# Lead-in of layer B: V tails staged in two tiles and stored by four transfers on SP, Q/K tails stored on SP alone

## The chip, the cores and the metric

The kernel runs on one core of one Trainium2 chip. The time is the device time of one execution in microseconds (us). The engines are TensorE (PE; its weight loads are shown apart as PEld), VectorE (DVE), ScalarE (ACT), GpSimd (POOL) and SyncE (SP). SP and ACT each have a queue on which they issue transfers (DMAs); the profile shows these as SPq and ACTq.

## What is computed

Four layers in a row, A, B, A, B, over 2048 tokens of width 640, each added to its input after a layernorm. This change touches only B, a recurrent attention with a memory of eight tokens:

```python
def _B_ref(x, mem0, Wq, Wk, Wv, Wo, seg_len):          # seg_len 32, 32 heads of 128
    mem = mem0                                           # 8 tokens
    for s in range(n_seg):                               # 64 segments
        xs = x[:, s * seg_len:(s + 1) * seg_len, :].copy()
        h = jnp.concatenate([mem, xs], axis=1)           # 40 tokens
        q, k, v = (einsum('btd,dhe->bhte', h, W) for W in (Wq, Wk, Wv))
        scores = einsum('bhqe,bhke->bhqk', q, k) * scale
        scores = jnp.where(mask[None, None], scores, -1000000000.0)
        o = einsum('bhqk,bhke->bhqe', softmax(scores), v)
        o = einsum('bhte,hed->btd', o, Wo)
        mem = o[:, :M, :].copy()                         # the next segment's memory
        outs.append(o[:, M:, :])
```

## The kernel before

Layer B (`layer_B`) works through 64 steps, one per segment, and each step needs the memory that the one before it made. A step multiplies 32 columns at a time: the eight memory tokens together with the first 24 tokens of the segment ("thin" products, `thin_mm`). The last eight tokens of each segment, the tails, don't depend on the memory. Their queries, keys and values are therefore made ahead, for eight segments at once, by sixteen units: eight for Q and K (`tail_unit`, `tail_evac`), eight for V (`vtail_unit`, `vtail_evac`). ACT or DVE evacuates a unit from PSUM into a staging tile in SBUF; the unit is then stored in DRAM, Q and K tails in `b_QKd`, V tails in `b_VTd`, and each step loads what it needs back, in the layout it needs: `b_tl` by one load (`tails_load`), which POOL then copies into `b_QZ` and `b_KT` (`tails_copy`), and the V tails by four loads into rows of `b_Vth` (`vtails_in`).

In the steady loop the units of the next eight segments are spread over eight steps. Ahead of the loop there is a lead-in (lines 983 to 1034), run once in each of the two B layers, that does all sixteen units of the first eight segments in a row:

- the layernorm of four groups of 128 tokens (`ln_load`, `ln_norm`), and their transposition into `b_HX` and `b_TX` (`ln_spread`: five transposes on PE into `b_lntps`, two copies on ACT);
- the eight Q/K units on PSUM tile `b_tail` (lines 997 to 1004), even ones evacuated by ACT and odd ones by DVE into `b_tu`, which stands in turn in four buffers of `b_kq` and in `b_QT`, `b_KT`, `b_tu` and `b_Vth`; even units are stored by ACT's queue, odd ones by SP's; `ln_spread` of the groups 2 and 3 stands after units 3 and 5;
- the thin products of step 0 (`b_Kp`, `b_Qp`), eight loads of the output weights `b_wo` on SP (640 KB each, line 1014), the transposes `b_TP`;
- the load of `b_tl` for step 0 (line 1021), which has to wait for all eight stores to `b_QKd`;
- the eight V units on PSUM tile `b_vtail` (lines 1024 to 1026), even ones evacuated by DVE and stored by SP, odd ones evacuated by ACT and stored by ACT; five are staged in one tile `b_vts` (the memory of `b_OTsb`), three in `b_vt` (the memory of `b_PTa`, `b_PTb` and `b_E`); each unit is stored by two transfers of 64 rows of 512 bytes;
- the thin product for V (`b_V`), the four loads of V tails into `b_Vth` (line 1030), and the first units of the next eight segments (lines 1032 to 1034).

Then step 0 begins with the thin products of step 1 (`b_Ka`, `b_Qa`, `b_Kb`, `b_Qb`), the transposes (`b_TPak` and so on), the scores of step 0 (`b_SP`), softmax, the product with V (`b_OTP`, which reads `b_Vth`) and the output projection (`b_OPS`, which reads `b_wo`).

The order on each engine is that of the program text: `_OrdNC` chains the instructions of PE, ACT, DVE and POOL, and ACT's stores stand in ACT's own order. SP's order is chosen by the scheduler of the framework. PSUM tiles of the lead-in share five buffers that go round (`ps_tile`), so a product may start only when the tile five before it has been evacuated. The framework gives every transfer of SP and ACT one of eight semaphores in turn; before a transfer is issued its queue waits until the last transfer with the same semaphore has landed.

`OTdef` are two tiles of 128 x 32 x 32 in which POOL collects the memory rows of `b_OTsb` at the end of every step, four steps per tile.

Of the kernel before, what the change touches and what calls it, by code (L numbers as in the profile page):

```python
# [19 lines left out]
BF16 = mybir.dt.bfloat16  # L20
# [756 lines left out]
def layer_B(nc, tc, C, W, x_src, xb_src, x_dst, mem0, B_Wv, B_Wo, nsteps=64, out_bf16=False, tag=""):  # L777
    SCB = 1.0 / math.sqrt(128.0)
    nc_raw = nc
    nc = _OrdNC(tc, nc_raw, engines=ORDER_ENGINES)  # L780
# [3 lines left out]
    VTd = tc.dram_tile([nsteps, 8, 4096], BF16, name=f"b_VTd{tag}")  # L784
    with ExitStack() as ctx:
        def pool(name, bufs):
            return ctx.enter_context(tc.tile_pool(name=name, bufs=bufs, reuse_waits="tile"))
# [6 lines left out]
        kqp = pool("b_kqp", 4)  # L794
        W.wo = pool("b_wo", 1).tile([128, 32, D], BF16, name="b_wo")
        st = pool("b_state", 1)
        w2 = pool("b_w2", 2)
        wk = pool("b_wk", 1)
# [8 lines left out]
        def ps_tile(shape, dtype, name):  # L807
            return pp.tile(shape, dtype, name=name, tag="ps")
# [7 lines left out]
        OTdef = [wk.tile([128, 32, 32], BF16, name=f"b_OTdef{i}") for i in range(2)]  # L816
# [12 lines left out]
        HX, TX, QT, KT, VH = {}, {}, {}, {}, {}  # L829
        ln_xt, ln_ready = {}, []  # L830

        def evac(eng, dst, src, scale=None):
            if eng == "act":
                if scale is None:
                    nc.scalar.copy(dst, src)
                else:
                    nc.scalar.activation(out=dst, in_=src, func=ACT.Copy, scale=scale)
            else:
                if scale is None:
                    nc.vector.tensor_copy(dst, src)  # L840
                else:
                    nc.vector.tensor_scalar(out=dst, in0=src, scalar1=scale, scalar2=None, op0=ALU.mult)
# [7 lines left out]
        def ln_norm(g):  # L850
            xt = ln_xt[g]
            f = layernorm_tile(nc, sml, C, xt[:], xt[:], "b_ln")
            if g in (0, 2) and not entered:
                info = mybir.DependencyInfo(mybir.DependencyClass.NoSync, mybir.DependencyReason.SCHED_ONLY)
                tc.add_manual_dep(f.ins, (C.after2 if g else C.after).ins.name, info, reason="order")
            ln_ready.append(g)

        def ln_spread(g):
            xt = ln_xt.pop(g)
            tps = ps_tile([128, NCH, 4, 32], BF16, "b_lntps")  # L860
            for c in range(NCH):
                nc.tensor.transpose(tps[:, c, :, :].rearrange("p i t -> p (i t)"), xt[:, 128 * c:128 * c + 128], C.identb[:])
            HX[g] = hp.tile([128, NCH, 4, 32], BF16, name="b_HX", tag="HX")
            T, half = divmod(g, 2)
            if half == 0:
                TX[T] = tx.tile([128, NCH, 8, 8], BF16, name="b_TX", tag="TX")
            nc.scalar.copy(TX[T][:, :, 4 * half:4 * half + 4, :], tps[:, :, :, 24:32])
            nc.scalar.copy(HX[g][:, :, :, 8:32], tps[:, :, :, 0:24])

        def cols_of(u):  # L870
            if u == nsteps:
                return HXz[:, :, 0, :]
            return HX[u // 4][:, :, u % 4, :]

        def thin_mm(cols_ap, Wt, b, name):
            ps = ps_tile([128, 512], F32, name)
            for c in range(NCH):
                for j in range(4):
                    n = 4 * b + j
                    nc.tensor.matmul(ps[32 * j:32 * j + 32, :], lhsT=cols_ap[:, c, :], rhs=Wt[:, c, 512 * n:512 * n + 512],  # L880
                                     start=(c == 0), stop=(c == NCH - 1), tile_position=(0, 32 * j), skip_group_check=True)
            return ps
# [30 lines left out]
                nc.sync.dma_start(VH[s - 1][32 * j:32 * j + 8, :, :],  # L913
                                  VTd[s].rearrange("t (b n e) -> t n b e", b=2, e=512)[:, j, :, :])

        tail_ps, vts = {}, {}

        def tail_unit(T, k, i0, i1, shared=False):
            proj, hg = divmod(k, 4)
            Wt = W.wk if proj else W.wq  # L920
            if i0 == 0:
                if shared:
                    tail_ps[0] = ps_tile([128, 8, 64], F32, "b_tail")
                else:
                    tail_ps[0] = po.tile([128, 8, 64], F32, name="b_tail", tag="tail")
            ps = tail_ps[0]
            for i in range(i0, i1):
                h = 8 * hg + i
                for c in range(NCH):
                    nc.tensor.matmul(ps[:, i, :], lhsT=Wt[:, c, 128 * h:128 * h + 128], rhs=TX[T][:, c, :, :].rearrange("p s t -> p (s t)"),  # L930
                                     start=(c == 0), stop=(c == NCH - 1))

        def tail_evac(T, k, eng, home=None, dma=nc.sync.dma_start):
            proj, hg = divmod(k, 4)
            pool_, tg = home or (wk, "tu")
            tu = pool_.tile([128, 8, 8, 8], BF16, name="b_tu", tag=tg)
            evac(eng, tu[:].rearrange("p s h t -> p h s t"), tail_ps[0][:].rearrange("p h (s t) -> p h s t", t=8),
                 None if proj else SCB)
            o = 256 * proj + 64 * hg
            dma(QKd[8 * T:8 * T + 8, :, o:o + 64].rearrange("s p f -> p s f"), tu[:].rearrange("p s h t -> p s (h t)"))  # L940

        def vtail_unit(T, k, c0=0, c1=NCH, ps=None):
            b4, ch = divmod(k, 2)
            if ps is None:
                ps = ps_tile([128, 256], F32, "b_vtail")
            for c in range(c0, c1):
                for q in range(4):
                    n = 2 * b4 + q // 2
                    nc.tensor.matmul(ps[32 * q:32 * q + 32, :], lhsT=TX[T][:, c, 4 * (q % 2):4 * (q % 2) + 4, :].rearrange("p s t -> p (s t)"),
                                     rhs=W.wv[:, c, 512 * n + 256 * ch:512 * n + 256 * ch + 256],  # L950
                                     start=(c == 0), stop=(c == NCH - 1), tile_position=(0, 32 * q), skip_group_check=True)
            return ps

        def vtail_evac(T, k, ps, eng, home=None, dma=nc.sync.dma_start):
            b4, ch = divmod(k, 2)
            if isinstance(home, int):
                if home == 0:
                    vts[0] = wk.tile([128, 5, 256], BF16, name="b_vts", tag="OTsb")
                vt = vts[0][:, home, :]
            else:  # L960
                pool_, tg = home or (wk, "vt")
                vt = pool_.tile([128, 256], BF16, name="b_vt", tag=tg)[:]
            evac(eng, vt, ps[:])
            for jj in range(2):
                o = 512 * (2 * b4 + jj) + 256 * ch
                dma(VTd[8 * T:8 * T + 8, :, o:o + 256].rearrange("s t f -> (s t) f"), vt[64 * jj:64 * jj + 64])
# [29 lines left out]
                nc.sync.dma_start(HX[0][:, c, 1, 0:8], mem0[:, 128 * c:128 * c + 128].rearrange("t p -> p t"))  # L996
        for k in range(8):
            tail_unit(0, k, 0, 8, shared=True)
            tail_evac(0, k, "act" if k % 2 == 0 else "dve", (((kqp, "kq"),) * 4 + ((w2, "QT"), (w2, "KT"), (wk, "tu"), (w2, "Vth")))[k],
                      (nc.sync if k % 2 else nc.scalar).dma_start)  # L1000
            if k in (0, 2) and n0 > 2:
                ln_norm(2 + k // 2)
            if k in (3, 5) and ln_ready:
                ln_spread(ln_ready.pop(0))
        cols = cols_of(0)
        jobs = [(nm, b) for b in range(2) for nm in ("K", "Q")]
# [1 line left out]
        for nm, b in jobs:  # L1008
            ps = thin_mm(cols, W.wk if nm == "K" else W.wq, b, f"b_{nm}p")
# [10 lines left out]
        XO, XOd = init_state()  # L1020
        tails_copy(0, tails_load(0))
        Vth = VH[-1] = w2.tile([128, 2, 512], BF16, name="b_Vth", tag="Vth")
        vt_homes = [0, 1, 2, 3, 4] + [(wk, x) for x in ("PTa", "PTb", "E0")]
        for k in range(8):
            vtail_evac(0, k, vtail_unit(0, k), "dve" if k % 2 == 0 else "act", vt_homes[k],
                       (nc.scalar if k % 2 else nc.sync).dma_start)
        for b in range(2):
            ps = thin_mm(cols, W.wv, b, "b_V")
            evac("act" if b == 0 else "dve", Vth[:, b, :], ps[:])
        vtails_in(0)  # L1030
        if NT > 1:
            tail_unit(1, 0, 0, 8, shared=True)
            tail_evac(1, 0, "act")
            vtail_evac(1, 0, vtail_unit(1, 0), "dve")
# [52 lines left out]
        for s in range(nsteps):  # L1087
# [139 lines left out]
            PTa = wk.tile([128, 2, 4, 40], BF16, name="b_PTa", tag="PTa")  # L1227
            ptpb = p_transp(1)
            PTb = wk.tile([128, 2, 4, 40], BF16, name="b_PTb", tag="PTb")
# [10 lines left out]
            OTsb = wk.tile([128, 32 * 40], BF16, name="b_OTsb", tag="OTsb")  # L1240
# [30 lines left out]
            if not last:  # L1271
                dst = cols_of(u + 1)
# [14 lines left out]
            if unit:  # L1287
                vtail_evac(unit[0], unit[1], vps, "act")
# [113 lines left out]
```

## Time and profile before

| what | value |
|---|---|
| median of the three runs shown | 2696.44 us (2691.12 to 2700.09) |
| the profiled execution's own time | 2692.14 us |
| its span in the profile | 2690.4 us |
| mean granted PE clock | 0.997 |
| PE busy | 2576.7 us, 96% of the span |
| DMA moved | 156.37 MB, mean 58 GB/s |

The page gives, for one profiled execution, the busy time of each engine, the chain of work that ended last, and the costliest groups. The timeline view lists instructions as "start us, us, engine, line, operation, out<-in, count", and in brackets the time the engine stood idle ahead of them and what ended it. The two B layers begin near 343 us and 1683 us of the span; their lead-ins end near 382 and 1722 us, where `b_Ka` of the loop begins. Line numbers of helpers stand for many instructions (L109 is the recorder through which nearly all of B's instructions go), so the tile names are what to go by.

### The profile page before, as it was taken

Reading aid. Unit: us, or ns where it says so; the run is one execution under the profiler, and the core shown is the slowest. Engines: PE = TensorE matmul, PEld = TensorE weight load, DVE = VectorE, ACT = ScalarE, POOL = GpSimd, SP = SyncE. Lnnn points to the kernel's source line nnn. Section 1 sums busy time; section 2 is a strip of 40 time slices with the busy share of each in tenths; the row PEclk is TensorE's granted clock in tenths of the full one; section 3 lists DMA queues with packets and bytes.
Section 4 is the critical chain, followed back from the end, with each engine's and each line's share of the span. In section 5 each row is a group of like instructions: output and inputs, shape, how many; then the busy total and the mean of one; then the engine's idle time right before and its main releaser. Section 6 shows DMA issues by size and latency. Waiting matters only on the chain.

```text
span 2690.4 us, 147288 instructions
## 1 busy us (share of the span) xinstructions
PE 2576.7 (96%) x65632; PEld 1699.2 (63%) x65632; DVE 1698.4 (63%) x4562; ACT 1583.1 (59%) x3718; POOL 710.0 (26%) x1631
## 2 busy tenths in 40 slices
PE   7999989999999999999989999899999999999998
PEld 5556566666666666666655566666666666666665
DVE  8999845555555555555589998455555555555554
ACT  6988835454555555554479898355555555555543
POOL 5777611111111111111156776111111111111110
PEclk9999999999999999999999999999999999999999
DMA  4122451222222222121120113511212121211110
GB/s 155 45 79 80 139 166 41 44 44 43 44 45 43 45 43 44 41 41 31 54 89 22 61 51 138 164 40 40 43 39 44 41 43 41 42 40 41 38 26 19
DMA packets 326620, 156.37 MB, mean 58 GB/s; under 512 B 246240, under 2 KB 310880, under 8 KB 324192
## 3 DMA queue, kind: packets, MB, share of 16 engines
q1 hardware_dynamic: 316384, 145.38, 21.3%
q8 instruction: 513, 8.40, 1.4%
q10 hardware_dynamic: 9600, 1.57, 0.4%
q14 instruction: 123, 1.01, 0.1%
HBM read 95.15 MB, written 51.71 MB: 55 GB/s over the span
## 4 chain that ended last, share of the span: by engine, by line
PE 79%; DVE 11%; ACT 5%; DMA 2%; issue 2%; SPq 1%; POOL 0%; ACTq 0%; DVEq 0%; POOLq 0%
PE b_OPS L109 11%; PE b_tail L109 5%; DVE a_nm L138 5%; PE b_Qa L109 5%; PE b_Ka L109 5%; PE b_Kb L109 5%; PE b_Qb L109 5%; PE b_Va L109 5%; PE b_Vb L109 5%; PE b_SP L109 4%; PE b_OTP L109 4%; PE b_OPSd L109 3%; PE b_PTP L109 3%; PE b_vtail L109 3%; ACT a_PT L138 3%; PE a_S L109 2%
## 5 line engine op out<-in xcount | busy, mean ns | idle before, releaser
L109 PEld LDWEIGHTS <-b_HX 128*32 128x32 bf16 x15360 | 427.9, 97 | 343.0 <-issue 12.4
L109 POOL TENSOR_TENSOR b_Pm<-b_E,b_rs 128x96 bf16<-128x96 bf16 x128 | 63.6, 497 | 1430.7 <-ACT b_Vth L109 1079.3
L138 DVE TENSOR_REDUCE a_nm<-a_S 128x2 f32<-128x512 f32 (+3 forms) x512 | 394.9, 815 | 27.6 <-PE a_S L109 20.1
L138 ACT ACTIVATE a_PT<-a_T 128x1024 bf16<-128x1024 f32 (+1 forms) x384 | 344.3, 901 | 32.0 <-PE a_T L109 24.2
L109 PE MATMUL b_OPS<-b_wo,b_OTsb 128*32 128x320 bf16 x8192 | 309.5, 301 | 10.4 <-issue 7.6
L109 PEld LDWEIGHTS <-b_OTsb 128*32 128x32 bf16 x8192 | 202.0, 97 | 95.7 <-DVE b_OTsb L109 24.3
L109 DVE CAST b_HX<-b_MT 128x8 bf16<-128x8 f32 x372 | 63.8, 172 | 274.2 <-PE b_MT L109 269.3
L138 POOL TENSOR_SCALAR_AFFINE_SELECT a_PT<-a_PT 128x256 bf16<-128x256 bf16 x380 | 188.7, 505 | 128.5 <-ACT a_PT L138 127.2
L109 ACT CAST b_msb<-b_OPS 128x64 bf16<-128x64 f32 x378 | 69.4, 256 | 237.7 <-PE b_OPS L109 237.6
L109 ACT CAST b_kq<-b_Kb 128x512 bf16<-128x512 f32 x128 | 75.0, 586 | 202.6 <-PE b_Kb L109 202.6
L109 DVE COPY b_KT<-b_TPak 128x128 bf16<-128x128 bf16 x128 | 28.8, 225 | 228.8 <-PE b_TPak L109 228.8
L109 DVE TENSOR_SCALAR b_kq<-b_Qa 128x512 bf16<-128x512 f32 x128 | 88.6, 692 | 130.3 <-PE b_Qa L109 127.2
L109 PE MATMUL b_Ka<-b_wk,b_HX 128*32 128x512 bf16 x2520 | 160.1, 381 | 6.2 <-ACT b_vt L109 6.2
L109 PE MATMUL b_Va<-b_wv,b_HX 128*32 128x512 bf16 x2520 | 161.0, 380 | 0.0
L109 PE MATMUL b_Qa<-b_wq,b_HX 128*32 128x512 bf16 x2520 | 159.9, 381 | 1.1 <-ACT b_Vth L109 1.1
L109 PEld LDWEIGHTS <-b_kq 128*128 128x128 bf16 x2080 | 116.9, 98 | 68.8 <-ACT b_kq L109 55.6
L109 PE MATMUL b_Vb<-b_wv,b_HX 128*32 128x512 bf16 x2520 | 160.3, 379 | 0.0
L109 PE MATMUL b_Kb<-b_wk,b_HX 128*32 128x512 bf16 x2520 | 159.5, 380 | 0.0
L109 PE MATMUL b_Qb<-b_wq,b_HX 128*32 128x512 bf16 x2520 | 158.8, 379 | 0.0
L109 DVE CAST b_OTsb<-b_OTP 128x160 bf16<-128x160 f32 (+1 forms) x384 | 122.5, 374 | 39.7 <-PE b_OTP L109 39.5
L109 ACT ACTIVATE b_E<-b_SP 128x320 bf16<-128x320 f32 (+1 forms) x256 | 81.1, 368 | 108.8 <-PE b_Va L109 100.0
L109 PE MATMUL b_vtail<-b_wv,b_TX 128*32 128x256 bf16 x2880 | 136.9, 271 | 3.9 <-issue 3.9
(211 smaller groups left out, 5786.1 us busy)
## 6 DMA issues: line engine op xcount, KB each, us to landing
b_tl<-b_QKd SPq DMA_DIRECT2D x128, 128.0 KB
b_QKd<-b_tu SPq DMA_DIRECT2D x120, 128.0 KB
b_wv<-in_B_Wv_dram SPq DMA_DIRECT2D x10, 1024.0 KB
b_wo<-in_B_Wo_dram SPq DMA_DIRECT2D x16, 640.0 KB
b_Vth<-b_VTd SPq DMA_DIRECT2D x512, 16.0 KB
b_XO<-xres SPq DMA_DIRECT2D x256, 30.0 KB
b_VTd<-b_vt SPq DMA_DIRECT2D x228, 32.0 KB
xres<-a_xnew SPq DMA_DIRECT2D x19, 320.0 KB
```

Of the source, the lines that this page charges most:

```text
L109: r = f(*a, **k)
L138: r = f(*a, **k)
```

## The change

Three things, all in the lead-in:

1. V tails: units 0 to 3 are staged in `OTdef[0]` and units 4 to 7 in `OTdef[1]`, each in its quarter of 256 columns. After units 3 and 7 two transfers of 64 rows (two pieces of 1024 bytes per row) are issued on SP: four stores of 64 KB in all. The tiles `b_vts` and the borrowed homes go.
2. Q/K tails: all eight stores are issued on SP. ACT issues no transfers any more.
3. `ln_spread` of the groups 2 and 3 stands after units 5 and 7.

In the built program SP's order in the lead-in becomes: one load of `b_wo`, the eight `b_QKd` stores, seven loads of `b_wo`, the load of `b_tl`, the four V stores, the load of `b_tl` for step 1, the first `b_QKd` store of the next eight segments, the four loads of `b_Vth`, the two V stores of that next unit, then two loads each of `b_XO` and `b_XOd`. Before, it was: one `b_wo`, two `b_QKd`, one `b_wo`, one `b_QKd`, one `b_wo`, one `b_QKd`, five `b_wo`, `b_tl`, eight V stores, `b_tl`, one `b_XO`, four `b_Vth`, one `b_QKd`, two V stores, one `b_XO`, two `b_XOd`; in the second B layer the three single `b_wo` stand a little differently among the four `b_QKd`. The orders of DVE and POOL don't change but for the names of the tiles; PE's differs only by the two groups of transposes.

```diff
-        tail_ps, vts = {}, {}
+        tail_ps = {}
...
         def vtail_evac(T, k, ps, eng, home=None, dma=nc.sync.dma_start):
             b4, ch = divmod(k, 2)
-            if isinstance(home, int):
-                if home == 0:
-                    vts[0] = wk.tile([128, 5, 256], BF16, name="b_vts", tag="OTsb")
-                vt = vts[0][:, home, :]
-            else:
-                pool_, tg = home or (wk, "vt")
-                vt = pool_.tile([128, 256], BF16, name="b_vt", tag=tg)[:]
+            if home is not None:
+                vt = OTdef[k // 4][:].rearrange("p a c -> p (a c)").rearrange("p (k f) -> p k f", f=256)[:, k % 4]
+                evac(eng, vt, ps[:])
+                if k % 4 == 3:
+                    src = OTdef[k // 4][:].rearrange("p a c -> p (a c)").rearrange("p (b f) -> p b f", f=512)
+                    dst = VTd[0:8, :, 512 * (k - 3):512 * (k + 1)].rearrange("s t (b j f) -> j (s t) b f", b=2, j=2)
+                    for jj in range(2):
+                        nc.sync.dma_start(dst[jj], src[64 * jj:64 * jj + 64])
+                return
+            vt = wk.tile([128, 256], BF16, name="b_vt", tag="vt")[:]
             evac(eng, vt, ps[:])
...
             tail_unit(0, k, 0, 8, shared=True)
-            tail_evac(0, k, "act" if k % 2 == 0 else "dve", (((kqp, "kq"),) * 4 + ((w2, "QT"), (w2, "KT"), (wk, "tu"), (w2, "Vth")))[k],
-                      (nc.sync if k % 2 else nc.scalar).dma_start)
+            tail_evac(0, k, "act" if k % 2 == 0 else "dve", (((kqp, "kq"),) * 4 + ((w2, "QT"), (w2, "KT"), (wk, "tu"), (w2, "Vth")))[k])
             if k in (0, 2) and n0 > 2:
                 ln_norm(2 + k // 2)
-            if k in (3, 5) and ln_ready:
+            if k in (5, 7) and ln_ready:
                 ln_spread(ln_ready.pop(0))
...
-        vt_homes = [0, 1, 2, 3, 4] + [(wk, x) for x in ("PTa", "PTb", "E0")]
         for k in range(8):
-            vtail_evac(0, k, vtail_unit(0, k), "dve" if k % 2 == 0 else "act", vt_homes[k],
-                       (nc.scalar if k % 2 else nc.sync).dma_start)
+            vtail_evac(0, k, vtail_unit(0, k), "dve" if k % 2 == 0 else "act", 0)
```

## The prediction

> **What bounds the kernel now.** I read the page first, for the share of each engine in the chain that ended last, then that chain, the timeline and windows around the two places that the diff touches.
>
> ```profile
> span 2690.4 us, 147288 instructions
> PE 79%; DVE 11%; ACT 5%; DMA 2%; issue 2%; SPq 1%; POOL 0%; ACTq 0%; DVEq 0%; POOLq 0%
> ```
>
> The PE holds 79% of the chain, so what the lead-ins of the two B layers are worth is what the PE idles or crawls in them. The chain inside the first lead-in (start, us, what):
>
> ```profile
> 371.99 8.02 DMA b_wo<-in_B_Wo_dram
> 380.08 0.45 ACTq L109
> ...
> 381.23 0.38 ACT b_vt L109
> 381.65 2.32 PE b_Ka L109 x20
> ...
> 387.83 1.08 PE b_Qb L109 x20
> ...
> 390.04 0.82 PE b_SP L109 x65
> ```
>
> It leaves the PE for a load of output weights, whose landing lets a store on ACT's queue go (`ACTq`), behind which ACT evacuates the last V tail at 381.23. The timeline shows the PE's side:
>
> ```profile
> 376.71 0.73 PE L109 MATMUL b_vtail<-b_wv,b_TX 128*32 128x256 bf16 x20
> ...
> 381.65 0.62 PE L109 MATMUL b_Ka<-b_wk,b_HX 128*32 128x512 bf16 x4 [4.21 <-ACT b_vt L109]
> ```
>
> The PE stands for 4.21 us, because `b_Ka` needs the PSUM buffer of that V tail. ACT's order is evacuation, two stores, evacuation, two stores; each DMA of the program carries one of eight semaphores in turn and waits until the transfer that held it before has landed. The stores of tail 5 got the semaphore of a 640 KB `b_wo` load. Windows (us, busy of PE, PEld, DVE, ACT, POOL, granted PE clock, DMA share, GB/s) add a second price:
>
> ```profile
> 361.00:369.00 8.00, 7.97 (x186) 5.25 (x185) 3.16 (x7) 3.38 (x7) 0.00 (x0) 1.00 1.26 238
> 374.00:380.00 6.00, 3.44 (x88) 2.72 (x81) 1.12 (x2) 0.37 (x1) 0.00 (x0) 1.00 1.06 375
> 381.00:387.00 6.00, 5.35 (x52) 2.36 (x55) 0.69 (x1) 2.04 (x4) 0.87 (x3) 0.50 0.23 61
> 387.50:395.00 7.50, 7.24 (x198) 4.83 (x190) 4.13 (x14) 4.77 (x12) 1.31 (x4) 1.00 0.28 60
> 392.00:393.00 1.00, 1.00 (x26) 0.43 (x15) 0.68 (x4) 0.91 (x3) 0.00 (x0) 1.00 0.82 125
> ```
>
> After the standstill the PE runs at a clock of 0.50 until about 387. The next step shows the same work at full clock:
>
> ```profile
> 399.33 1.25 PE L109 MATMUL b_Ka<-b_wk,b_HX 128*32 128x512 bf16 x20
> ...
> 404.98 0.28 PE L109 MATMUL b_SP<-b_KT,b_QT 128*32 128x40 bf16 x16
> ...
> 409.79 0.52 PE L109 MATMUL b_OTP<-b_PTa,b_Vth 32*128 32x40 bf16 x32
> ```
>
> From `b_Ka` to the scores it is 404.98 - 399.33 = 5.65 us there and 390.04 - 381.65 = 8.39 us in the lead-in: 2.74 us lost to the clock. The second lead-in, 1340 us later:
>
> ```profile
> 1719.52 0.73 PE L109 MATMUL b_vtail<-b_wv,b_TX 128*32 128x256 bf16 x20
> ...
> 1722.27 1.26 PE L109 MATMUL b_Ka<-b_wk,b_HX 128*32 128x512 bf16 x20 [2.02 <-ACT b_vt L109]
> 1723.29 0.40 POOL L109 COPY b_KT<-b_tl 128x256 bf16<-128x256 bf16 x1
> 1724.61 1.26 PE L109 MATMUL b_Qa<-b_wq,b_HX 128*32 128x512 bf16 x20 [1.08 <-ACT b_Vth L109]
> 1729.00 2.86 SPq L913 DMA_DIRECT2D b_Vth<-b_VTd x4
> 1733.95 0.47 PE L109 MATMUL b_OTP<-b_PTa,b_Vth 32*128 32x40 bf16 x32
> ```
>
> Here ACT is late for two PSUM buffers, 2.02 and 1.08 us, and `b_Ka` takes 1.26, the full-clock time.
>
> **The change part by part.**
>
> *ACT issues no stores any more.* Sixteen V-tail stores of 32 KB (eight on ACT) become four of 64 KB on SP, and the four `b_QKd` stores of ACT move to SP. ACT's evacuations then stand in a row with nothing but the PE ahead of them; in the changed program their other waits are for transfers issued before 357.2 and, for `b_kq`, for the first `b_QKd` stores, which now precede seven of the eight weight loads. So the waits named above go: 4.21 + 2.74 in the first lead-in, 2.02 + 1.08 in the second, 10.05 together.
>
> *The two `ln_spread` move two units later* (after units 5 and 7 instead of 3 and 5).
>
> ```profile
> 357.32 2.49 PE L109 MATMUL b_tail<-b_TX,b_wk 128*128 128x64 bf16 x80 [1.54 <-ACT b_tu L109]
> 359.65 0.44 PE L109 MATMUL b_lntps<-c_identb,b_xt 128*128 128x128 bf16 x5
> ...
> 1701.73 0.67 DVE L109 TENSOR_SCALAR b_tu<-b_tail 128x512 bf16<-128x512 f32 x1
> 1701.86 0.45 PE L109 MATMUL b_lntps<-c_identb,b_xt 128*128 128x128 bf16 x5 [1.53 <-DVE b_xt L109]
> ...
> 1702.45 2.49 PE L109 MATMUL b_tail<-b_TX,b_wk 128*128 128x64 bf16 x80
> 1704.88 1.26 PE L109 MATMUL b_Kp<-b_wk,b_HX 128*32 128x512 bf16 x20
> ```
>
> The PSUM buffers go round in five. At 357.32 the PE has waited 1.54 us for ACT to free one; in the changed order one more unit (40 matmuls, 2.49 / 2 = 1.25 us) has a free buffer and runs inside this wait, in the place of five transposes (0.44): 0.8 us won. In the second lead-in the 1.53 us behind the late `b_xt` are filled by unit 6, but unit 7 needs the buffer that DVE frees at 1701.73 + 0.67 = 1702.40; unit 7 and the transposes after it end at about 1704.0, not 1704.88: 0.9 us. Bounds: 0 (another wait takes it) to 1.5 each; I take 0.8 and 0.9, worked out buffer by buffer.
>
> *SP gets the whole queue.* Its order becomes: one `b_wo`, eight `b_QKd` stores, seven `b_wo`, the tails `b_tl`, four V stores, the next `b_tl`, a `b_QKd` store, four `b_Vth` loads. Three things are queued behind and can be late: `b_tl` (POOL copies it into `b_KT` before the scores), `b_Vth` (needed by `b_OTP`), `b_wo`.
>
> ```profile
> 357.31 0.38 SPq L768 DMA_DIRECT2D b_wo<-in_B_Wo_dram  x1
> ...
> 360.13 2.05 ACTq L109 DMA_DIRECT2D b_QKd<-b_tu  x1
> 361.14 2.08 SPq L768 DMA_DIRECT2D b_wo<-in_B_Wo_dram  x1
> ...
> 365.79 0.86 SPq L940 DMA_DIRECT2D b_QKd<-b_tu  x1
> ...
> 382.67 0.40 POOL L109 COPY b_KT<-b_tl 128x256 bf16<-128x256 bf16 x1
> 388.19 2.85 SPq L913 DMA_DIRECT2D b_Vth<-b_VTd x4
> 395.04 0.47 PE L109 MATMUL b_OTP<-b_PTa,b_Vth 32*128 32x40 bf16 x32
> ```
>
> What the transfers need: a weight load is 655 KB at 375 GB/s, 1.75 us; a `b_QKd` store 131 KB, by the window at 392 (125 GB/s at share 0.82) 0.86 to 1.05 us. Eight of each are 20.9 to 22.4 us; from 357.31 they end at 378.2 to 379.7 if the DMA never runs dry, and it has nine transfers queued by then. `b_tl` follows with 0.35 us; two copies of POOL end in `b_KT`. Today that copy ends at 382.67 + 0.40 = 383.07; I expect 380 to 383, and take 381.9. Without any wait the scores would come 7.75 us earlier (4.21 + 2.74 + 0.8), at 382.3: just covered, and what is lost if it isn't is the difference. `b_Vth`: after the copy come one `b_tl`, one `b_QKd` (about 0.4 each) and 2.85 us of issuing; in the second lead-in `b_OTP` starts at 1733.95, 1733.95 - 1731.86 = 2.1 us after the last issue ended, so landing takes no more than 2.1. Sum: copy + 5.8 at most, 387.7, against 382.3 + 4.8 (409.79 - 404.98) = 387.1 for `b_OTP`. I charge 0.5 us. In the second lead-in the copy ends today at 1723.69; +5.8 is 1729.5, and `b_OTP` without waits falls at 1733.95 - 4.0 = 1729.95: covered.
>
> The share of 1.26 in 361 to 369, with both queues at work, against 1.06 with nearly only SP's, speaks against this: 8 x (1.26 - 1.06) = 1.6 us of transfers overlapped that one queue may string out. The Trainium skill (DMA: Bandwidth & Descriptors, "Issuing engines are not separate DMA queues") says that all issuing engines share the same DMA engines and that several of them save only the sequencer's time; by it nothing is strung out and the sum stands. By the row it would be a rival, below. I take the sum, since the share can also rise when small packets of one queue wait on each other.
>
> Staging in `OTdef` costs nothing: POOL first writes these tiles at the end of step 0, long after the stores.
>
> Sum: 4.21 + 2.74 + 0.8 - 0.5 = 7.25 and 2.02 + 1.08 + 0.9 = 4.0, together 11.25 us. The profiled execution took 2692.14 us (1.74 around its span), so 2680.9; the median of the runs shown, 2696.44, lies 4.30 above it, so 2685.2, rounded 2685.
>
> **The rivals.**
>
> *One queue strings the transfers out* by 1.6 us (row above). Copies end at 384.7 and 1725.3, `b_OTP` at 390.5 instead of 395.04 and 1731.1 instead of 1733.95: a gain of 4.5 + 2.9 = 7.4, 2689. For it: the shares. Against it: 374 to 380 moves 375 GB/s with SP nearly alone.
>
> *The weight loads come too late (slower).* Seven of them now wait behind all eight stores.
>
> ```profile
> 1699.94 0.74 SPq L768 DMA_DIRECT2D b_wo<-in_B_Wo_dram  x1
> 1707.09 0.48 SPq L940 DMA_DIRECT2D b_QKd<-b_tu  x1
> ```
>
> If the eighth store is issued no earlier than today, at 365.79 (1707.09 in the second lead-in), the second load moves from 361.14 to 366.65, 5.5 us, and from 1699.94 to 1707.57, 7.6 us, and everything behind it as far. First lead-in: copy at 388.6, `b_OTP` at 394.4, 0.6 won. But the PE would stand 388.6 - 382.3 = 6.3 us at the scores, longer than the 4.21 that brought the half clock, so another 2.7 is lost. Second: 1723.69 + 7.6 + 5.8 = 1737.1, 3.1 lost, and 2.7. Sum 7.9 slower: 2704. With one delay x in both it decides from 2.6 us on (6.2 - x + 4.45 - x - 5.4 = 0, the half clock counted). For it: issues of 2.05 and 2.08 us when the queue is full. Against: eight stores keep the DMA busy meanwhile, so a late issue isn't a late landing, and the eighth store was behind weight loads that now follow it. The Trainium skill (TensorE: Matmul & The Clock Gate, "Part 1: The HAM clock gate (the "warmup" mystery)") puts the fall to half clock at about 3.4 us without work; 4.21 here agrees.
>
> *Nothing moves:* another wait of the same length takes the PSUM buffers' place. 2696. Against it: the list of waits has none.
>
> **How the numbers follow.** Forecast 0.60, strung out 0.20, nothing 0.06, slower 0.14. 0.3% is 8.1 us, about what a measurement of this kernel can tell from no change. The forecast's own range is a gain of 8 to 14 with the runs' spread, 2679 to 2690; 2678 to 2695 takes in the strung-out case and half of nothing. Faster: 0.58 of the first case and 0.06 of the second, 0.64; slower: 0.09 of the last (delays beyond those worked out, or a stall at `b_OPS` as well); same: the rest, 0.27.
>
> **What would show it.** In the profile after: no ACTq issues; `b_Ka` starting within 0.5 us of the end of `b_vtail` in both lead-ins; clock 1.00 throughout; scores near 382 and 1725 on the shifted scale; POOL's `b_KT` copy ending before them. Wrong would be: a wait `b_SP` or `b_OTP` on POOL or a `b_Vth` load over 2 us, a clock of 0.50 anywhere there, or `b_OPS` waiting for `b_wo`.

## The result and the profile after

| | before | changed |
|---|---|---|
| median of 19 runs each | 2696.87 us (2690.71 to 2703.04) | 2688.34 us (2684.38 to 2692.05) |
| profiled execution | 2692.14 us | 2689.89 us |
| its span | 2690.4 us | 2688.1 us |

The ratio is 0.9968, 95% interval [0.9962, 0.9975]: 8.5 us less. Two later comparisons gave 0.9981 [0.9970, 0.9991] and 0.9984 [0.9973, 0.9996], 5.8 and 4.6 us less.

The page of the changed kernel: span, shares of the chain by engine, then two groups of the costliest instructions (busy us, mean ns of one, idle ahead of them and what ended most of it).

```profile
span 2688.1 us, 147188 instructions
...
PE 80%; DVE 11%; ACT 5%; issue 2%; DMA 2%; SPq 0%; POOL 0%; DVEq 0%; ACTq 0%; POOLq 0%
...
L109 PE MATMUL b_Ka<-b_wk,b_HX 128*32 128x512 bf16 x2520 | 159.0, 379 | 0.2 <-DVE b_HX L109 0.2
L109 PE MATMUL b_vtail<-b_wv,b_TX 128*32 128x256 bf16 x2880 | 137.4, 271 | 8.2 <-issue 8.1
```

The same two groups on the page of before:

```profile
L109 PE MATMUL b_Ka<-b_wk,b_HX 128*32 128x512 bf16 x2520 | 160.1, 381 | 6.2 <-ACT b_vt L109 6.2
...
L109 PE MATMUL b_vtail<-b_wv,b_TX 128*32 128x256 bf16 x2880 | 136.9, 271 | 3.9 <-issue 3.9
```

The 6.2 us that `b_Ka` waited for ACT (4.21 + 2.02 in the two lead-ins) are gone. `b_vtail` idles 4.3 us more over the whole execution, on nothing that the page can name ("issue"); 2.0 of them lie in the first lead-in, and what PE waits for there is worked out in the last section. The timeline of the first lead-in of the changed kernel:

```profile
356.62 0.72 ACT L382 CAST a_xnb<-a_xnew 128x640 bf16<-128x640 f32 x1 [3.12 <-DVE b_ln_st L109]
357.90 1.33 PE L109 MATMUL b_tail<-b_TX,b_wk 128*128 128x64 bf16 x40 [0.88 <-ACT b_tu L109]
...
374.50 0.50 PE L109 MATMUL b_vtail<-b_wv,b_TX 128*32 128x256 bf16 x9 [2.50 <-issue]
374.73 4.12 PE L109 MATMUL b_V<-b_wv,b_HX 128*32 128x512 bf16 x40
...
376.89 3.15 SPq L963 DMA_DIRECT2D b_VTd<-b_OTdef  x4
...
380.05 0.73 PE L109 MATMUL b_vtail<-b_wv,b_TX 128*32 128x256 bf16 x20
380.61 1.25 PE L109 MATMUL b_Ka<-b_wk,b_HX 128*32 128x512 bf16 x20
...
384.63 0.40 POOL L109 COPY b_KT<-b_tl 128x256 bf16<-128x256 bf16 x1
...
385.06 0.35 SPq L902 DMA_DIRECT2D b_tl<-b_QKd  x1
...
386.06 3.01 SPq L913 DMA_DIRECT2D b_Vth<-b_VTd  x4
...
386.23 0.28 PE L109 MATMUL b_SP<-b_KT,b_QT 128*32 128x40 bf16 x16
...
391.02 0.47 PE L109 MATMUL b_OTP<-b_PTa,b_Vth 32*128 32x40 bf16 x32
...
395.59 1.26 PE L109 MATMUL b_Ka<-b_wk,b_HX 128*32 128x512 bf16 x20
```

`b_Ka` follows the V tail at once, and from it to the scores it is 386.23 - 380.61 = 5.62 us, the full-clock time (8.39 before). But ahead of it there is a new gap of 2.50 us (0.49 before), and `b_V` takes 4.12 us (2.43 before). SP's issues of the V stores end at 376.89 + 3.15 = 380.04, and the next `b_tl` is issued only at 385.06, after POOL's copy; the `b_Vth` loads stand behind it. Windows of the same kernel, with the columns of before's:

```profile
361.00:369.00 8.00, 7.98 (x179) 5.19 (x179) 3.35 (x7) 3.17 (x7) 0.00 (x0) 1.00 1.05 172
374.50:377.90 3.40, 3.40 (x44) 2.61 (x48) 0.00 (x0) 0.96 (x2) 0.00 (x0) 0.58 1.07 364
380.00:387.00 7.00, 7.00 (x195) 4.31 (x194) 2.16 (x7) 3.62 (x8) 0.87 (x3) 1.00 0.64 204
...
1729.30:1732.50 3.20, 3.04 (x100) 2.02 (x104) 1.01 (x3) 0.75 (x2) 0.40 (x1) 0.63 0.16 36
```

The half clock has moved: not behind `b_Ka` any more, but 0.58 behind the new gap. The second lead-in, timeline:

```profile
1692.96 0.73 ACT L382 CAST a_xnb<-a_xnew 128x640 bf16<-128x640 f32 x1 [1.90 <-DVE b_ln_rstd L109]
...
1715.99 1.25 PE L109 MATMUL b_Ka<-b_wk,b_HX 128*32 128x512 bf16 x20
...
1722.85 0.40 POOL L109 COPY b_KT<-b_tl 128x256 bf16<-128x256 bf16 x1
...
1723.30 0.28 PE L109 MATMUL b_SP<-b_KT,b_QT 128*32 128x40 bf16 x16 [0.73 <-POOL b_KT L109]
...
1729.31 0.36 PE L109 MATMUL b_OTP<-b_PTa,b_Vth 32*128 32x40 bf16 x29 [0.75 <-DMA b_Vth<-b_VTd]
...
1730.12 4.03 PE L109 MATMUL b_OPS<-b_wo,b_OTsb 128*32 128x320 bf16 x64 [0.15 <-DVE b_OTsb L109]
...
1734.98 1.25 PE L109 MATMUL b_Ka<-b_wk,b_HX 128*32 128x512 bf16 x20
```

Here too `b_Ka` waits no more; but the Q/K tails (through POOL's copy) and the V tails land late, 0.73 and 0.75 us, and `b_OPS` runs at about half clock, 4.03 us for the 2.54 of other traces.

One profiled time shifts by several us between executions (spans of 2688.1, 2686.7 and 2681.0 for the changed kernel in three comparisons). So the traces are compared below by the length of each lead-in, from the start of the last `a_xnb` cast to step 1's `b_Ka`. In the changed kernel that is 395.59 - 356.62 = 38.97 us and 1734.98 - 1692.96 = 42.02 us. The ends of before that were not shown yet:

```profile
356.05 0.72 ACT L382 CAST a_xnb<-a_xnew 128x640 bf16<-128x640 f32 x1 [2.94 <-DMA xres_bf<-a_xnb]
...
1696.41 0.72 ACT L382 CAST a_xnb<-a_xnew 128x640 bf16<-128x640 f32 x1 [1.92 <-DVE b_ln_rstd L109]
...
1738.88 1.25 PE L109 MATMUL b_Ka<-b_wk,b_HX 128*32 128x512 bf16 x20
```

They make 399.33 - 356.05 = 43.28 and 1738.88 - 1696.41 = 42.47 us. All kernels, one value for each trace taken:

| kernel | lead-in 1, us | lead-in 2, us | ratio to before, 95% interval |
|---|---|---|---|
| before | 43.28 | 42.47 | 1 |
| changed | 38.97, 40.08, 37.90 | 42.02, 40.27, 39.47 | 0.9968, 0.9981, 0.9984 (above) |
| part 1 alone | 37.39, 38.33 | 37.89, 38.90 | 0.9969 [0.9957, 0.9981], 0.9973 [0.9962, 0.9985] |
| parts 2 and 3 | 42.11 | 44.21 | 0.9993 [0.9984, 1.0002] |
| parts 1 and 2 | 39.34 | 40.96 | 0.9990 [0.9980, 0.9999] |
| 16 V stores on SP, old tiles | 44.51 | 47.03 | 1.0025 [1.0016, 1.0033] |
| 16 V stores on SP, `OTdef` | 46.32 | 46.98 | 1.0024 [1.0015, 1.0034] |
| changed, `b_wo` late | 38.20, 37.93 | 37.77, 38.08 | 0.9952 [0.9939, 0.9964], 0.9966 [0.9952, 0.9979] |
| part 1, `b_wo` late | 40.27 | 40.25 | 0.9974 [0.9965, 0.9983] |
| before, `b_wo` late | 42.24 | 43.52 | 1.0019 [1.0009, 1.0029] |

Part 1 is the V staging, part 2 the Q/K stores on SP, part 3 the moved `ln_spread`.

### The profile page after: what moved, and what is told of

Read it like the earlier page. It is cut to its first block, busy times and chain, and to the rows that moved or that the text cites. A ratio compares the mean times of both kernels' runs of the same rounds, so it can differ in the third digit from the quotient of the medians.

```text
span 2688.1 us, 147188 instructions
## 1 busy us (share of the span) xinstructions
PE 2574.6 (96%) x65568; PEld 1700.1 (63%) x65632; DVE 1696.3 (63%) x4562; ACT 1583.6 (59%) x3718; POOL 707.4 (26%) x1631
## 4 chain that ended last, share of the span: by engine, by line
PE 80%; DVE 11%; ACT 5%; issue 2%; DMA 2%; SPq 0%; POOL 0%; DVEq 0%; ACTq 0%; POOLq 0%
PE b_OPS L109 11%; PE b_tail L109 6%; DVE a_nm L138 5%; PE b_Ka L109 5%; PE b_Qa L109 5%; PE b_Kb L109 5%; PE b_Qb L109 5%; PE b_Va L109 5%; PE b_Vb L109 5%; PE b_SP L109 4%; PE b_OTP L109 4%; PE b_vtail L109 3%; PE b_OPSd L109 3%; PE b_PTP L109 3%; ACT a_PT L138 3%; PE a_S L109 2%
```

## The experiments

**The parts alone.** Part 1 alone puts back into the changed kernel

```diff
             tail_evac(0, k, "act" if k % 2 == 0 else "dve", (((kqp, "kq"),) * 4 + ...)[k],
+                      (nc.sync if k % 2 else nc.scalar).dma_start)
...
-            if k in (5, 7) and ln_ready:
+            if k in (3, 5) and ln_ready:
```

and parts 2 and 3 have the old `vtail_evac`, the old homes and the stores alternating between SP and ACT.

> Part 1 of the change alone: V tails staged in OTdef, four stores on SP; the Q/K stores alternate between SP and ACT as before and ln_spread stands after units 3 and 5. If ACT's V stores ahead of its evacuations are what the change removes, b_Ka waits under 0.5 us for ACT in both lead-ins and the time falls by 6 to 9 us, to 2688 to 2691 (the change itself: 8.5). If the moved Q/K stores or ln_spread carry the gain, the time stays within 2 us of before, 2695 to 2698.

> Parts 2 and 3 alone: all Q/K stores on SP and ln_spread after units 5 and 7; the sixteen V stores and their staging as before, half of them on ACT. First theory: ACT still stands at its V stores, b_Ka or b_V waits 2 to 6 us for ACT in the first lead-in, the clock falls to 0.50 again, and the time is 2694 to 2699. Rival (parts 2 and 3 carry it): 2688 to 2690 and no wait on ACT.

Measured: 2677.65 us against 2686.95 of before in that comparison, -9.3 us, for part 1; 2686.11, -0.8 us and within its interval of nothing, for parts 2 and 3. So part 1 carries the whole gain. Its trace, first lead-in:

```profile
373.74 0.50 PE L109 MATMUL b_vtail<-b_wv,b_TX 128*32 128x256 bf16 x10 [0.55 <-issue]
373.97 2.43 PE L109 MATMUL b_V<-b_wv,b_HX 128*32 128x512 bf16 x40
...
377.60 0.73 PE L109 MATMUL b_vtail<-b_wv,b_TX 128*32 128x256 bf16 x20
378.16 1.24 PE L109 MATMUL b_Ka<-b_wk,b_HX 128*32 128x512 bf16 x18
380.21 0.39 PE L109 MATMUL b_Ka<-b_wk,b_HX 128*32 128x512 bf16 x2 [0.80 <-issue]
```

The gap ahead of `b_V` is 0.55 us and `b_V` runs at full clock; a second such gap, 0.80 us, lies inside `b_Ka`. In the trace of parts 2 and 3 `b_Ka` still waits for `ACT b_vt` (1.42 and 0.89 us) and `b_Qa` for ACT's next evacuation (1.33 and 1.50), less for `b_Ka` than the 2 to 6 us expected in lead-in 1; the fall of the clock came, but at `b_OPS` (4.03 us in both lead-ins).

**Number of stores and staging tiles.** Two kernels keep sixteen stores of 32 KB, all on SP: one out of the old tiles, one out of `OTdef`.

```diff
-            vtail_evac(0, k, vtail_unit(0, k), "dve" if k % 2 == 0 else "act", 0)
+            vtail_evac(0, k, vtail_unit(0, k), "dve" if k % 2 == 0 else "act", vt_homes[k])
```

```diff
-                if k % 4 == 3:
-                    src = ...
-                    dst = ...
-                    for jj in range(2):
-                        nc.sync.dma_start(dst[jj], src[64 * jj:64 * jj + 64])
+                for jj in range(2):
+                    o = 512 * (2 * b4 + jj) + 256 * ch
+                    nc.sync.dma_start(VTd[8 * T:8 * T + 8, :, o:o + 256]..., vt[64 * jj:64 * jj + 64])
```

> The change, but the V tails stay in their old staging tiles and go out in sixteen stores of 32 KB, all on SP. First theory (the queue matters, since a store on ACT holds back evacuations): b_Ka's wait for ACT is gone as in the change; twelve more stores of 0.59 us on SP put the b_Vth loads some 7 us later, so b_OTP waits 4 to 7 us in both lead-ins and most of the gain is given back there: 2692 to 2699. Rival (the number of stores doesn't matter): the time of the change, 2687 to 2690, and no wait of b_OTP over 1 us.

> The change, but with sixteen stores of 32 KB out of the same two OTdef tiles, all on SP: it splits the number of stores from the staging tiles. Theory N (more stores keep SP longer, about 12 x 0.4 to 0.6 us = 5 to 7 us more ahead of b_Vth): b_Vth issues 5 us later than with four stores, b_OTP waits 3 to 5 us in each lead-in, time 5 to 9 us above the change, ratio near 1.000. Rival H (in the kernel with sixteen stores from the old tiles the loss was the exponential b_E waiting 6.6 us for the last store out of the tile it takes over): with OTdef nothing takes the tile over, so b_E waits for no store, and the time is within 2 us of the change, ratio 0.996 to 0.998.

Measured: 2693.12 us against 2686.95, and 2702.10 against 2694.47: both slower than before. With the old tiles the list of waits of 370 to 400 us (total, times, longest) names the last tile's next owner, since `b_E` takes over a tile that a store still reads:

```profile
ACT b_E L109 <- DMA b_VTd<-b_vt: 6.6, 1, 6.6
```

That fits the rival of the second kernel, but with `OTdef` the loss is as large at another place. Its timeline:

```profile
377.40 14.04 SPq L961 DMA_DIRECT2D b_VTd<-b_OTdef  x16
391.61 3.10 SPq L913 DMA_DIRECT2D b_Vth<-b_VTd  x4
...
393.91 0.19 PE L109 MATMUL b_OTP<-b_PTa,b_Vth 32*128 32x40 bf16 x1 [3.50 <-DMA b_Vth<-b_VTd]
```

Sixteen issues keep SP 14.04 us, against 3.15 us for the four of the changed kernel; `b_Vth` is issued 5.5 us later than at 386.06 (not 10.9, since in the changed kernel SP stands until 385.06 anyway), and `b_OTP` waits for it four times, 5.3 us in all. The theory that counts stores held; the one that blames the tiles alone fell. Both kernels keep parts 2 and 3: there, taking ACT out of the V stores pays only because there are fewer of them. Sixteen stores on SP with four Q/K stores left on ACT were not measured.

**The changed kernel again**, in two more comparisons:

> The changed kernel once more, to set its first profile beside a second. Theory G (the gap of 2.50 us ahead of the last nine b_vtail matmuls and the half clock behind it, and in lead-in 2 the half clock at b_OPS, belong to the change): a gap of over 2 us and a window of clock near 0.6 at b_V again, 4 us for b_V x40, and a ratio of 0.9965 to 0.9970. Rival (the gap is chance of the one profiled run): a gap of 0.5 to 1.6 us, b_V x40 in 2.43 us, b_Ka right behind b_vtail and step 1's b_Ka some 4 us sooner after the lead-in's start (35 us after the last a_xnb cast, not 39), with the same ratio, as the median is over many runs.

> The changed kernel on the same chip as the next three: ratio 0.9965 to 0.9980 (5 to 9 us below before).

Measured: gaps ahead of the last `b_vtail` of 1.57 and 1.92 us, `b_V` at full clock both times, `b_Ka` right behind the tail but with a second gap of 0.80 us inside it. Half clock shows in the first of them at `b_OPS` of lead-in 1 (4.21 us), in the second in neither lead-in, and that trace has the shortest of both. The ratios, 0.9981 and 0.9984, lie above what either run was expected to give. So neither theory held whole: the gap belongs to the change, the half clock behind it comes in some executions.

**Part 3**, undone alone:

```diff
-            if k in (5, 7) and ln_ready:
+            if k in (3, 5) and ln_ready:
```

> The change without the moved layer norm spread (it stays behind tails 3 and 5). Theory as predicted (the move takes 0.8 and 0.9 us of waits of the tails): 1.7 us slower than the change, ratio near 0.9975, with b_tail waiting for ACT b_tu 1.5 us instead of 0.9. Rival (PE has slack there, since the weights' and wo loads decide what follows): within 0.5 us of the change.

Measured: 2692.16 us, 3.5 us above the changed kernel beside it, though the two intervals overlap. By the lead-ins the move is worth 39.34 - 38.98 and 40.96 - 40.59 (means of the changed kernel), 0.7 us together. The first kind of number has more noise, the second a single trace; a small gain is likely, its size is open. The move isn't quite undone alone either: in this kernel SP issues one `b_wo` load ahead of the eighth `b_QKd` store, and POOL's copy ends at 386.33. The wait that it shortens, without the move:

```profile
357.85 2.49 PE L109 MATMUL b_tail<-b_TX,b_wk 128*128 128x64 bf16 x80 [1.49 <-ACT b_tu L109]
```

**The `b_wo` loads.** SP issues eight loads of 640 KB ahead of `b_tl` and the V stores. Half of them were put behind the last V tail in the program text, in the changed kernel, in part 1 alone and in the kernel before (SP's own order is again the scheduler's: in the changed kernel two of the four then stand ahead of the V stores, one between and one behind them):

```diff
-        for k in range(8):
+        for k in range(4):
             load_B_wo(nc, W, B_Wo, k)
...
             vtail_evac(0, k, vtail_unit(0, k), ...)
+        for k in range(4, 8):
+            load_B_wo(nc, W, B_Wo, k)
```

> The change with the last four b_wo loads issued behind b_tl (three before it instead of seven). If the late landing of b_tl and b_Vth behind the weight loads is what the change still pays, POOL's b_KT copy ends 5 us or more earlier in both lead-ins, the waits of b_SP and b_OTP (0.7 us each in the second lead-in) go, and the time falls by 1 to 3 us against the change, 2685 to 2687. The gap of PE without a releaser (2.5 us in the first lead-in of the change) stays if it comes with transfers of weights at full rate, whatever their order; if it goes as well, 2683 to 2685.

> The change with the last four b_wo loads behind the last V tail, beside the change on one chip. If the 11.25 us of the sum were there and the change gives 3 to 5 us of them back to waits for b_KT and b_Vth behind SP's eight b_wo loads: 3 to 5 us below the change, ratio 0.9945 to 0.996. If the earlier difference was the chip's: within 1.5 us of the change.

> Part 1 alone, beside the whole change on one chip. If parts 2 and 3 give nothing: within 1.5 us of the change. If they cost (eight Q and K stores on SP put the copy b_tl and with it the V stores later, so that b_OTP waits 0.7 us for b_Vth): 2 to 4 us below the change, ratio 0.995 to 0.9965. If they give their 0.8 and 0.9 us: 1 to 2 us above the change.

> The V staging alone (tails' Q and K stores alternate between SP and ScalarE as before, layer norm spread not moved), and the last four b_wo loads issued behind the last V tail. Theory A (the V staging carries the gain, the other parts give nothing, the late b_wo loads give 3 us): about 3 us below the V staging alone and at most 1 us from the change with late b_wo loads, ratio 0.994 to 0.9955. Rival (with Q and K stores on ScalarE the copy b_tl is soon enough already, so late loads give nothing more): ratio 0.9965 to 0.9970.

> The kernel before with only the last four b_wo loads put behind the last V tail: the V stores stay sixteen, half of them on ScalarE. Theory W (ScalarE's V stores stand only because a b_wo load holds their semaphore): b_Ka waits for ACT b_vt 1 us or less in lead-in 1, ratio 0.996 to 0.9975. Rival Q (eight stores on ScalarE hold it anyway, since some take the semaphore of a V store or a b_wo load that is as late): b_Ka still waits over 2 us for ACT b_vt, and the ratio is 0.9985 to 1.002.

Measured: on the changed kernel 2674.75 us against 2686.95 (-12.2), then 2682.67 against 2692.10 (-9.4), the fastest kernel in both comparisons; its intervals still overlap those of part 1 alone. The second comparison has the changed kernel beside it, 4.9 us above, within the 3 to 5 expected. Part 1 alone came 1.7 us below the changed kernel on the same chip (2685.82 and 2687.55), also within the intervals. POOL's copy and `b_OTP` in the second of these traces with late loads:

```profile
377.69 0.40 POOL L109 COPY b_KT<-b_tl 128x256 bf16<-128x256 bf16 x1
...
390.06 0.47 PE L109 MATMUL b_OTP<-b_PTa,b_Vth 32*128 32x40 bf16 x32
```

The copy comes 7 us sooner than at 384.63, and the scores wait for it in no lead-in of the two traces. PE's gap ahead of the last `b_vtail` stays, 1.64 and 1.38 us. For part 1 the late loads gave nothing: 2689.56 against 2694.47, -4.9 us. There SP's order still had all four late loads ahead of the V stores: loads from 375.34, V stores from 378.94 and 381.18, `b_Vth` only from 388.25 (385.44 in the first trace of part 1 alone), and `b_OTP` of lead-in 1 waited four times for `b_Vth`, 0.5 us each.

The kernel before with late loads got slower, 2697.61 against 2692.10. The signs split: in lead-in 1 `b_Ka` waits for no V tail, as theory W said, but the ratio, 1.0019, is that of rival Q. Its trace shows what held ACT:

```profile
373.14 3.38 ACTq L109 DMA_DIRECT2D b_VTd<-b_vts  x2
376.57 0.37 ACT L109 CAST b_vts<-b_vtail 128x256 bf16<-128x256 f32 x1 [5.27 <-DMA b_VTd<-b_vts]
...
382.51 0.37 ACT L109 CAST b_vt<-b_vtail 128x256 bf16<-128x256 f32 x1 [3.08 <-DMA b_VTd<-b_vt]
```

Its evacuations still stand behind ACT's own stores, now up to 5.27 us; PE waits 1.72 us at `b_V` and 1.94 at `b_Qa` in lead-in 1, 1.84 at `b_tail` and 3.12 at `b_Ka` in lead-in 2. In its built program the two stores ahead of the 5.27 us of lead-in 1 wait on semaphores that `b_wo` loads hold, the two ahead of the 3.08 us on those of earlier V stores of ACT itself. So the run did not take the weight loads out of ACT's way, but it shows that ACT stands without one as well: what costs is stores with such waits standing between evacuations. The lead-ins of this trace balance to nothing, so they don't explain its whole 5.5 us.

## Why the prediction came out as it did

The time is within the range, 3.3 us above the forecast, and the mechanism of its largest term is as forecast. The size is less sure than that: the stated gain was 8 to 14 us, the three comparisons gave 8.5, 5.8 and 4.6, and the lead-ins show 6.2 us of the 11.25 of the sum. That the first comparison lies inside the range is in part luck.

- *ACT issues no stores (10.05 us).* Right in place, and nearly in size: part 1 alone shortens the lead-ins by 5.4 and 4.1 us (means of two traces against the one of before), 9.5 together, where 6.95 and 3.10 were forecast, so the total fits better than its halves. All the waits named are gone, and the half clock behind `b_Ka` with them. The account of what held ACT, a weight load on the semaphore, fits tail 5 of the kernel before but was too narrow: with late loads, earlier V stores held it as well.
- *`ln_spread` (0.8 and 0.9 us).* The wait fell from 1.54 to 0.88, not to nothing, and undoing the move cost 0.7 us in the lead-ins, less than half of the 1.7 forecast.
- *SP gets the whole queue (0.5 us charged).* This is the step that failed in size. Parts 1 and 2 without 3 have lead-ins 1.5 and 2.6 us longer than part 1 alone, some 4 us where 0.5 were charged (beside the old V staging, parts 2 and 3 together lengthen them by only 0.6). The sum let the stores and weight loads end at 378.2 to 379.7 "if the DMA never runs dry"; its share was 0.62 in 358 to 360 and 0.83 in 368 to 370, `b_tl` behind them landed at 384.17, and POOL's `b_KT` copy ended at 385.03, past the bound of 383. In lead-in 1 something else had delayed the scores by then: with the shift of 0.57 us between the traces taken off they came 390.04 - 385.66 = 4.4 us sooner, not 7.75. The gap (2.50 - 0.49 = 2.0), a wait that the sum has no term for, and the half clock at `b_V` (4.12 - 2.43 = 1.7) cover that difference. In lead-in 2, called covered, the copy cost 0.73 and `b_Vth` 0.75 us, and `b_OPS` 1.5 us at half clock.
- *`OTdef` costs nothing.* No trace shows a wait for a transfer out of these tiles.
- *The sum.* Part 1 at 9.5, part 2 at -4, part 3 at 0.7 give 6.2 us, as they must, being differences between the same traces; it is what the changed kernel has on average over its three (4.3 + 1.9). Most kernels here have one trace, and the changed kernel's own three differ by 2.2 and 2.6 us, so the split among the parts is rough.
- *The rivals.* The slower one needed an issue of `b_tl` 2.6 us late in both lead-ins with a stall at the scores; those stalls were 0 and 0.73 us. "One queue strings the transfers out" came nearest in time, 2689, and in its signs: on the scale of before (shifts between the traces, 0.57 and -3.45 us, taken off) the copies end at 384.5 and 1726.7, where it has 384.7 and 1725.3, and `b_OTP` begins at 390.5 and 1731.5, where it has 390.5 and 1731.1. Its share fell as well, from 1.26 to 1.05 in 361 to 369, while part 1 alone keeps 1.26 and has its copies end at 383.2 and 1723.8 on that scale. So 1.3 and 2.9 us of lateness come with parts 2 and 3. But in lead-in 1 the scores began 1.2 us after the copy had ended: there the time of `b_OTP` was set by the gap and the half clock, and the match is luck. The mix of transfers in the window differs too (stores first, weights later), so the runs don't say whether the queue or the order lowered the share, and the rule of the Trainium skill (DMA: Bandwidth & Descriptors, "Issuing engines are not separate DMA queues") is not refuted by it.
- *What would show it.* Of the signs named, "clock 1.00 throughout" failed, and a clock of about 0.50, named as a sign of being wrong, was seen; the scores came at 385.7 and 1726.8 on the scale of before, not near 382 and 1725. The waits for POOL and `b_Vth` stayed under the 2 us that were named as wrong. The fall to half clock was tied to an idle time like the 4.21 us of before; here it followed a gap of 2.50. The Trainium skill (TensorE: Matmul & The Clock Gate, "Part 1: The HAM clock gate (the "warmup" mystery)") puts it at about 3.4 us without work; in this trace less was enough.

## What to carry to other kernels

In this kernel stores issued by an engine that also evacuates PSUM made PE wait for DMA completions; fewer, larger stores on a queue that nobody computes on freed it, but with the same number of stores on that queue the issuing took 14.04 us instead of 3.15, the loads behind it came 5.5 us later, and the gain was gone. Moving a transfer costs what then stands behind it: here the order on the one queue, small urgent transfers ahead of large weights not needed yet, gave the fastest kernel measured in both comparisons it stood in. A stretch at half clock appears in some executions and not in others, so compare a stage over several traces before a us of it is explained.

## What the runs showed of the hardware

The page of the changed kernel has an instruction queue among its DMA queues (packets, MB, share), and counts PE's instructions:

```profile
PE 2574.6 (96%) x65568; PEld 1700.1 (63%) x65632; DVE 1696.3 (63%) x4562; ACT 1583.6 (59%) x3718; POOL 707.4 (26%) x1631
...
q8 instruction: 513, 8.40, 1.4%
```

- PE's gaps with no releaser are waits for its own instructions, as far as the traces can show it. The 513 packets are of 16 KB each, one for every 256 of PE's matmuls and weight loads. Where a lead-in shows two such gaps in a row, 128 matmuls, with their weight loads, lie between them. The timelines of 356 to 400 and 1690 to 1745 of the fourteen traces list fifty gaps of this kind, and by the traces' records of DMA packets each of them ends 1.26 to 1.60 us after a packet of this queue has landed.
- The gap ahead of the last `b_vtail` matmuls of lead-in 1 goes with part 2: 1.32 to 2.50 us in the nine traces that have all Q/K stores on SP, 0.49 to 0.84 us in the five that don't. The packet ahead of it takes about 1 us in both groups, but lands 4.3 to 5.4 us after the first `b_vtail` matmul in the nine and 3.4 to 3.7 us in the five. In lead-in 2 the groups overlap (gaps of 0.36 to 1.93 us against 0 to 0.72). Around the gap the DMAs move some 365 GB/s at a share above 1 in both groups (window 374 to 380 of before, 375 GB/s). Why the packet lands later with part 2 is not shown.
- The granted clock fell to half after a gap of 2.50 us (changed kernel), and not after one of 2.04 us (parts 1 and 2), 1.93 us (first repeat, lead-in 2) or 1.92 us (second repeat). At `b_OPS` of the changed kernel it fell behind a wait for `b_Vth` of 0.71 to 0.75 us in two lead-ins, and in five lead-ins of other kernels where the last of several such waits was 0.41 to 0.99 us; it stayed full behind 0.67, 0.83 and 0.86 us in three others. The length of the last wait alone doesn't tell.
